# Part B of a fused attention and state-space kernel: queues written out by a list schedule, both magnitude tables of a chunk together, tiles laid out without shared ranges

## The chip, the cores and the metric

The kernel runs on one core of a Trainium2 chip. The metric is device time in microseconds (us) of one execution. The engines are TensorE (PE, with its weight loads as PEld), VectorE (DVE), ScalarE (ACT), GpSimd (POOL) and SyncE (SP, which here only issues DMAs). Each engine takes its instructions in the order of its own queue; an instruction that waits holds up all that stand behind it in the same queue.

## The reference, cut to what matters

Two independent parts are computed from their own inputs and laid side by side in the output (2048 rows, 640 + 640 columns).

```
part A (x: 2048 x 640, 32 heads of 20):
  q, k, v = x @ wqkv
  logits[s, w] = q[s] . k[s - 2w] / sqrt(20)      w = 0..7, masked where s < 2w
  out_a = softmax(logits) applied to v[s - 2w], then @ wo

part B (u: 2048 x 640, state size N = 192):
  dt = exp(log_dt);  K[d, l] = Re sum_n C[d,n] * exp(dt*A[d,n]*l) * dt*B[d,n]     l = 0..2047
  out_b = causal convolution of u with K along l, by an FFT of 4096  +  u * Dskip
```

## The kernel before, in words

Part B works on five chunks `c` of 128 channels. The start (`prep_dt`, `prep_coef`, `prep_chunk`) turns the parameters into logarithms and angles, splits them into pairs of half-precision pieces, writes these to a scratch tensor in memory (`scr`) and reads them back in another layout as PF (frequency pieces) and PM (magnitude pieces, `load_pieces`).

For each chunk and each half `th` of it, `table_steps` (L185) makes the powers exp(dt*A*l): PE multiplies the pieces by constant matrices into PSUM (L203, L206), and ACT turns each PSUM tile into a table. These are one small tile E (`gens`, Exp, L216), three tiles M (`mag`, Exp, L224), two tiles MX (`magx`, Exp, L238), and twelve tiles of 128 x 1024 for Y and X (`sin`, Sin, L252). Exp and Sin need different tables of ACT, and each change is an ACT_TABLE_LOAD. DVE multiplies M and MX by E (L229, L240), and Y and X by M and MX (L258 to L260, L264). M, MX and E have one buffer each; Y and X have one for each half.

`kgen_steps` (L274) then forms 16 of the chunk's 32 columns of K: 256 small matmuls into one PSUM tile (L290, L294), copied out by ACT (L297). With both halves done, `fwd_steps` does the forward transform of K (first stage L381, second stage L392). `prod` (L420) multiplies it by the transform of u, which the same `fwd_steps` made earlier and which lies in memory as `Ud`. `inv_steps` (L429) does the first inverse stage and stores it as `Zd`. Each step of these leaves a PSUM tile of 128 x 1024 that ACT or DVE copies to SBUF (L342, class `Evac`: a fixed pattern of letters says which engine takes which). Per chunk there are 20 such copies when a transform of u falls into it, and 2 of `kgen`.

The order comes from `interleave` (L347): it deals two lists of steps into each other in proportion to their lengths. One list is the table steps of the next half, the other what is left of this half: `kgen`, the inverse stage of the chunk before, and a forward transform. All PSUM tiles of part B come from one pool of four buffers of 128 x 1024 (tag `b`, L447). `InOrder` (L28) keeps a few chains of instructions in written order; for the rest the compiler's own scheduler orders each engine's queue.

The second inverse stage of part B (`ib`, L569) comes last, mixed with part A. It loads `Zd` back in groups of 12 of the 64 values of `l` (L575, five DMAs to a group, two buffers in turn) and multiplies by the constant H, loaded once (L564). Part A (`Attention`) starts within part B's last chunk: x is loaded and transposed (L637), then k and q of the first half are projected (L657) while the last chunk is finished. `Attention.run` (L796) does the rest: logits, softmax, the products with v (L772, L776) interleaved with `ib`, and the output projection (L790).

Of the kernel before, what the change touches and what calls it, by code (L numbers as in the profile page):

```python
# [10 lines left out]
A = mybir.AluOpType  # L11
# [7 lines left out]
NCH = 5  # L19
# [8 lines left out]
class InOrder:  # L28

    def __init__(self, tc):  # L30
        self.tc = tc; self.prev = None
    def __call__(self, ins):
        if self.prev is not None:
            self.tc.add_manual_dep(ins.ins, self.prev.name, mybir.DependencyInfo(mybir.DependencyClass.NoSync, mybir.DependencyReason.DATA), reason="act_order")
        self.prev = ins.ins
# [9 lines left out]
def load_dt(tc, pools, prm):  # L45
    nc = tc.nc
    pool = pools["arena"]
    ldt = pool.tile([128, NCH], bf16, name="ldt")
    lsrc = prm["B_log_dt"].rearrange("(g c t) -> g t c", g=4, c=NCH, t=32)
    for g in range(4):  # L50
        nc.scalar.dma_start(out=ldt[32 * g:32 * g + 32, :], in_=lsrc[g])
    return ldt


def prep_dt(tc, pools, ldt, order):
    nc = tc.nc
    pool = pools["arena"]
    dt = pool.tile([128, NCH], bf16, name="dt")
    order(nc.scalar.activation(out=dt[:], in_=ldt[:], func=ACT.Exp))
    dts = pool.tile([128, 3, NCH], f32, name="dts")  # L60
    nc.vector.tensor_scalar(out=dts[:, 0], in0=dt[:], scalar1=ASC, scalar2=None, op0=A.mult)
    nc.vector.tensor_scalar(out=dts[:, 1], in0=dt[:], scalar1=TURN, scalar2=None, op0=A.mult)
    order(nc.scalar.activation(out=dts[:, 2], in_=dt[:], func=ACT.Ln))
    return dts


def prep_coef(tc, pools, nat, lndt, n, order, vorder, T):

    nc = tc.nc
    V = nc.vector  # L70
    W = [128, n, CW]
    Br, Bi, Cr, Ci = (nat[:, a] for a in range(4))

    def zed():
        vorder(V.tensor_tensor(out=T[:, 0], in0=Br, in1=Cr, op=A.mult))
        vorder(V.tensor_tensor(out=T[:, 2], in0=Bi, in1=Ci, op=A.mult))
        V.tensor_tensor(out=T[:, 0], in0=T[:, 0], in1=T[:, 2], op=A.subtract)
        vorder(V.tensor_tensor(out=T[:, 1], in0=Br, in1=Ci, op=A.mult))
        vorder(V.tensor_tensor(out=T[:, 3], in0=Bi, in1=Cr, op=A.mult))
        V.tensor_tensor(out=T[:, 1], in0=T[:, 1], in1=T[:, 3], op=A.add)  # L80
        nc.scalar.activation(out=T[:, 2:4], in_=T[:, 0:2], func=ACT.Square)
        V.tensor_tensor(out=T[:, 4], in0=T[:, 2], in1=T[:, 3], op=A.add)

    def logs():
        order(nc.scalar.activation(out=T[:, 2:5], in_=T[:, 2:5], func=ACT.Ln, bias=pools["tiny"][:]))
        V.tensor_tensor(out=T[:, 3], in0=T[:, 3], in1=T[:, 2], op=A.subtract)
        V.scalar_tensor_tensor(out=T[:, 4], in0=T[:, 4], scalar=0.5, in1=lndt.unsqueeze(2).to_broadcast(W), op0=A.mult, op1=A.add)
        V.scalar_tensor_tensor(out=T[:, 2], in0=T[:, 3], scalar=-1.0, in1=T[:, 3], op0=A.mult, op1=A.max)

    def exps():  # L90
        order(nc.scalar.activation(out=T[:, 2], in_=T[:, 2], func=ACT.Exp, scale=-0.5))
        nc.scalar.activation(out=T[:, 3], in_=T[:, 3], func=ACT.Sign)
        nc.scalar.activation(out=T[:, 0:2], in_=T[:, 0:2], func=ACT.Sign, bias=pools["tiny"][:])

    def angle():
        ang = T[:, 2]
        order(nc.scalar.activation(out=ang, in_=ang, func=ACT.Arctan))
        V.scalar_tensor_tensor(out=ang, in0=ang, scalar=PI / 4, in1=T[:, 3], op0=A.subtract, op1=A.mult)
        V.scalar_tensor_tensor(out=ang, in0=ang, scalar=PI / 4, in1=T[:, 0], op0=A.add, op1=A.mult)
        V.scalar_tensor_tensor(out=ang, in0=ang, scalar=PI / 2, in1=T[:, 1], op0=A.subtract, op1=A.mult)  # L100
    return zed, logs, exps, angle, T[:, 4], T[:, 2]


def prep_chunk(tc, S1, S2, Are, Aim, dts, lam, ang, c, scr, vorder, sorder):


    nc = tc.nc
    V = nc.vector
    p = c % 2
    b1, tk, tq, b2 = S1[:, 3 * p:3 * p + 3], S1[:, 6], S1[:, 7], S1[:, 8]  # L110
    pc1, pc2, pc3 = (S2[:, 10 * p + a:10 * p + b] for a, b in ((0, 6), (6, 8), (8, 10)))
    so = sorder if sorder is not None else (lambda x: None)

    def frac(out, x, q):
        V.tensor_scalar(out=tk, in0=x, scalar1=1.0 / q, scalar2=MAGIC, op0=A.mult, op1=A.add)
        V.tensor_scalar(out=tk, in0=tk, scalar1=MAGIC, scalar2=q, op0=A.subtract, op1=A.mult)
        V.tensor_tensor(out=out, in0=x, in1=tk, op=A.subtract)

    def base():
        vorder(V.tensor_scalar(out=b1[:, 1], in0=Are, scalar1=dts[:, 0, c:c + 1], scalar2=-60000.0, op0=A.mult, op1=A.max))  # L120
        vorder(V.tensor_scalar(out=tq, in0=Aim, scalar1=dts[:, 1, c:c + 1], scalar2=None, op0=A.mult))
        frac(b1[:, 0], tq, 65536.0)
        frac(b1[:, 2], b1[:, 0], 1024.0)
        nc.scalar.copy(out=pc1[:, 0:3], in_=b1)
        vorder(V.tensor_tensor(out=pc1[:, 3:6], in0=b1, in1=pc1[:, 0:3], op=A.subtract))
        so(nc.sync.dma_start(out=scr[c, 0:6].rearrange("k p n -> p k n"), in_=pc1))

    def logmag():
        nc.scalar.copy(out=pc2[:, 0], in_=lam)
        vorder(V.tensor_tensor(out=pc2[:, 1], in0=lam, in1=pc2[:, 0], op=A.subtract))  # L130
        so(nc.sync.dma_start(out=scr[c, 6:8].rearrange("k p n -> p k n"), in_=pc2))

    def phi():
        V.tensor_scalar(out=tq, in0=b1[:, 0], scalar1=31.5, scalar2=None, op0=A.mult)
        V.scalar_tensor_tensor(out=tq, in0=ang, scalar=-TURN, in1=tq, op0=A.mult, op1=A.add)
        frac(b2, tq, 65536.0)
        nc.scalar.copy(out=pc3[:, 0], in_=b2)
        V.tensor_tensor(out=pc3[:, 1], in0=b2, in1=pc3[:, 0], op=A.subtract)
        so(nc.sync.dma_start(out=scr[c, 8:10].rearrange("k p n -> p k n"), in_=pc3))
    return base, logmag, phi  # L140


def new_pieces(tc, pools):


    nc = tc.nc
    PF = pools["arena"].tile([128, 8, CW], f16, name="PF", tag="PF", bufs=2)
    PM = pools["arena"].tile([128, 8, CW], f16, name="PM", tag="PM", bufs=2)
    nc.gpsimd.memset(PF[32:64], 0.0)
    nc.gpsimd.memset(PF[32:33], 4096.0)  # L150
    nc.gpsimd.memset(PM[64:128], 0.0)
    return PF, PM


def load_pieces(tc, P, scr, c, parts, sorder=lambda x: None):
    nc = tc.nc
    PF, PM = P
    where = {0: [(1, PM, 0), (4, PM, 1), (0, PF, 0), (3, PF, 1), (2, PF, 4), (5, PF, 5)], 1: [(6, PM, 2), (7, PM, 3)], 2: [(8, PF, 6), (9, PF, 7)]}
    for p in parts:
        for k, t, r in where[p]:  # L160
            sorder(nc.sync.dma_start(out=t[16 * r:16 * r + 16], in_=scr[c, k].rearrange("(g t) n -> t g n", t=16)))
# [22 lines left out]

def table_steps(tc, pools, R, P, th, order, Y, X, rows=(128, 128), vorder=None):  # L185

# [3 lines left out]
    nc = tc.nc  # L190
    V = nc.vector
    MM = nc.tensor.matmul
    RF, RM = R
    PF, PM = P
    pool, psp = pools["arena"], pools["psum"]
    M = pool.tile([128, 6400], bf16, name="M", tag="M", bufs=1)
    MX = pool.tile([128, 24, 32, 4], bf16, name="MX", tag="MX", bufs=1)
    E = pool.tile([128, 2, 24, 4], bf16, name="E", tag="E", bufs=1)
    steps = []

    def block(ps, blk, Pt, rhs, K=128):
# [7 lines left out]
    def new():  # L209
        return psp.tile([128, 2, 512], f32, name="ps_t", tag="b", bufs=4)  # L210

    def gens():
        ps = new()
        for blk in range(6):
            block(ps[:, 0, 32 * blk:32 * blk + 32], blk, PM, RM[:, 768:800], rows[0])
        order(nc.scalar.activation(out=E[:].rearrange("p k (b q) t -> p b k (q t)", b=6), in_=ps[:, 0, 0:192].rearrange("p (b k t) -> p b k t", k=2, t=16), func=ACT.Exp))  # L216

    def mag(b):
        def run():
            ps = new()  # L220
            for q in range(2):
                for i in range(2):
                    block(ps[:, q, 256 * i:256 * i + 256], 2 * b + i, PM, RM[:, 256 * q:256 * q + 256], rows[0])
# [8 lines left out]
    def magx(b0, n):  # L232
        def run():
            ps = new()
            for i in range(n):
                block(ps[:, i // 2, 256 * (i % 2):256 * (i % 2) + 256], b0 + i, PM, RM[:, 512:768])
# [656 lines left out]
```

## Time and profile before

| what | us |
|---|---|
| median of 3 runs (lowest, highest) | 533.36 (531.23, 533.85) |
| the profiled execution, whole | 537.6 |
| its span, first to last instruction | 535.8 |
| PE, DVE, ACT busy in the span | 391.0, 389.2, 345.4 |
| mean granted TensorE clock | 0.895 of full |

In this profile an instruction group is named by its line, engine, operation and tiles; "busy" is the union of its spans; "idle before" is time in which that engine stood still just before the group, with the instruction that ended it (the releaser). "issue" as a releaser means that the engine waited for nothing that the profile shows. A table of busy time by stretches of the span is the view that gives the stages: up to 52 us the start; 52 to 108 the first chunk; 108.17 to 344.20 the other four chunks; 344 to 383 the last transforms beside the first projections of part A; then part A with the last inverse stage.

### The profile page before, as it was taken

The page shows a single profiled execution, that of the slowest core. Times are in us where ns is not written, and L with a number is a line of the kernel's source. Part 1 is how long each engine was busy: PE and PEld are TensorE (multiplying, and loading weights), DVE is VectorE, ACT ScalarE, POOL GpSimd, SP SyncE. Part 2 cuts the span into 40 slices and gives each one's busy share as a digit, 9 for nine tenths or more (in the row PEclk, how much of TensorE's full clock was granted, in tenths as well). Part 3 has the DMA queues.
Part 4 walks back from the last instruction along what each step waited for, and adds up shares of the span by engine and source line. Part 5 has one row for each costly group of instructions (what it writes and reads, how often), then busy time and mean ns, then how long its engine had stood idle before and what let it go on. Part 6 is the DMA issues. An engine that isn't in the chain of part 4 may idle for free.

```text
span 535.8 us, 15507 instructions
## 1 busy us (share of the span) xinstructions
PE 391.0 (73%) x7009; PEld 245.8 (46%) x7009; DVE 389.2 (73%) x420; ACT 345.4 (64%) x451; POOL 35.9 (7%) x51
## 2 busy tenths in 40 slices
PE   0214675856798858976897678799799797788687
PEld 0103553533475436643564356445444465455355
DVE  3656997938878596989885977704585999985840
ACT  2393795957889868986998669557345362633254
POOL 8700001010002001010000000000000000000000
PEclk9999877878899887988799789989999799877879
DMA  5499343280028100750016008902102004653413
GB/s 122 107 156 220 115 139 84 94 195 3 1 67 260 31 0 18 234 166 1 3 44 196 1 2 295 241 22 80 80 1 62 1 4 113 188 123 103 102 67 107
DMA packets 51706, 51.57 MB, mean 96 GB/s; under 512 B 37416, under 2 KB 48360, under 8 KB 48696
## 3 DMA queue, kind: packets, MB, share of 16 engines
q1 hardware_dynamic: 49752, 49.69, 34.3%
q0 software_dynamic: 1184, 0.89, 0.8%
q8 instruction: 55, 0.90, 0.7%
q10 hardware_dynamic: 704, 0.00, 0.1%
q14 instruction: 11, 0.09, 0.1%
HBM read 32.30 MB, written 18.19 MB: 94 GB/s over the span
## 4 chain that ended last, share of the span: by engine, by line
DVE 36%; PE 34%; ACT 15%; issue 10%; DMA 4%; ACTq 0%; SPq 0%; POOL 0%; DVEq 0%; POOLq 0%
PE ps_qk L657 6%; DVE A L342 4%; DVE Y L258 4%; PE ps_t L203 4%; PE ps_k L290 4%; DVE X L264 3%; DVE prod L772 3%; PE ps_k L294 3%; DVE Y L260 3%; ACT Y L252 3%; PE ps_op L790 3%; PE ps_ia L429 2%; ACT X L252 2%; DVE Ssp L342 2%; DVE prod L713 2%
## 5 line engine op out<-in xcount | busy, mean ns | idle before, releaser
L252 ACT ACTIVATE X<-ps_t 128x1024 bf16<-128x1024 int16 x60 | 61.5, 1055 | 4.8 <-PE ps_t L203 3.3
L252 ACT ACTIVATE Y<-ps_t 128x1024 bf16<-128x1024 int16 x60 | 61.0, 1045 | 5.5 <-PE ps_t L203 3.5
L772 DVE TENSOR_TENSOR prod<-v,attn 128x2048 bf16<-128x2048 bf16 (+1 forms) x48 | 47.4, 1041 | 15.3 <-PE ps_o L776 15.3
L203 PE MATMUL ps_t<-R,PF 128*128 128x512 f16 (+1 forms) x160 | 52.0, 415 | 1.7 <-ACT Ksb L297 0.6
L713 DVE TENSOR_TENSOR prod<-qT,kT 128x5120 bf16<-128x5120 bf16 x16 | 44.6, 2817 | 9.1 <-ACT qT L342 4.7
L203 PE MATMUL ps_t<-R,PM 128*128 128x256 f16 (+3 forms) x160 | 22.9, 272 | 36.5 <-DMA PM<-scr 23.5
L258 DVE TENSOR_TENSOR Y<-Y,M 128x2048 bf16<-128x2048 bf16 x30 | 36.6, 1220 | 15.4 <-ACT Y L252 15.4
L342 DVE CAST A<-ps_f 128x1024 bf16<-128x1024 f32 x28 | 34.1, 1219 | 15.8 <-PE ps_f L381 15.8
L342 ACT CAST Ssp<-ps_f 128x1024 bf16<-128x1024 f32 x26 | 26.5, 1019 | 19.4 <-PE ps_f L392 19.4
L294 PE MATMUL ps_k<-Y,X 64*32 64x64 bf16 x1280 | 26.5, 235 | 16.5 <-issue 16.5
L264 DVE TENSOR_TENSOR X<-X,MX 128x2048 bf16<-128x2048 bf16 x30 | 36.6, 1219 | 0.2
L260 DVE TENSOR_TENSOR Y<-Y,M 128x2048 bf16<-128x2048 bf16 x30 | 36.6, 1218 | 0.2
L776 PE MATMUL ps_o<-prod,ident 32*32 32x512 bf16 (+1 forms) x768 | 24.1, 388 | 14.8 <-DVE prod L772 12.3
L381 PE MATMUL ps_f<-BD,u 128*64 128x128 bf16 x320 | 21.8, 290 | 17.5 <-DMA BD<-c_BD 12.0
L203 PEld LDWEIGHTS <-PM 128*128 128x128 f16 (+1 forms) x160 | 13.9, 102 | 44.4 <-DMA PM<-scr 23.5
L294 PEld LDWEIGHTS <-X 64*32 64x32 bf16 x1280 | 19.9, 116 | 30.1 <-issue 29.5
L381 PEld LDWEIGHTS <-u 128*64 128x64 bf16 x320 | 19.7, 204 | 25.5 <-issue 25.5
L224 ACT ACTIVATE M<-ps_t 128x1024 bf16<-128x1024 f32 x30 | 28.5, 1026 | 3.9 <-DVE Y L260 3.9
L420 DVE TENSOR_TENSOR U<-U,Ssp 128x2048 bf16<-128x2048 bf16 x20 | 24.3, 1221 | 9.0 <-ACT Ssp L342 9.0
L392 PE MATMUL ps_f<-A,WK 128*128 128x128 bf16 x160 | 16.5, 265 | 18.2 <-DVE A L342 18.2
L290 PE MATMUL ps_k<-Y,X 128*32 128x64 bf16 x1280 | 24.4, 242 | 5.7 <-ACT Ssp L342 1.9
L206 PE MATMUL ps_t<-R,PF 128*64 128x512 f16 (+1 forms) x160 | 27.4, 433 | 1.7 <-ACT Ssp L342 0.9
(146 smaller groups left out, 795.0 us busy)
## 6 DMA issues: line engine op xcount, KB each, us to landing
Udram<-Ssp SPq DMA_DIRECT2D x5, 1024.0 KB
U<-Udram SPq DMA_DIRECT2D x5, 1024.0 KB
U<-Udram SPq DMA_DIRECT2D x10, 512.0 KB
Zdram<-Z SPq DMA_DIRECT2D x5, 1024.0 KB
zq<-Zdram SPq DMA_DIRECT2D x25, 192.0 KB
u<-in_B_u_dram SPq DMA_DIRECT2D x4, 640.0 KB
xn<-in_A_x_dram SPq DMA_DIRECT2D x4, 640.0 KB
out_dram<-ob SPq DMA_DIRECT2D x16, 160.0 KB
```

Of the source, the lines that this page charges most:

```text
L203: MM(ps, lhsT=Pt[0:K, 2 * blk + th, 0:128], rhs=rhs[0:K], start=True, stop=True, skip_group_check=True)
L252: order(nc.scalar.activation(out=dst, in_=ps[:].bitcast(i16)[:, :, 0::2].rearrange("p i (k z) -> p (i k) z", z=128), func=ACT.Sin, scale=S ...
L258: V.tensor_tensor(out=hi, in0=lo, in1=m(0), op=A.mult)
L260: V.tensor_tensor(out=lo, in0=lo, in1=m(1), op=A.mult)
L264: V.tensor_tensor(out=xf, in0=xf, in1=mx, op=A.mult)
L290: MM(o, lhsT=X[:, r, 4 * g + t // 4, :, t % 4], rhs=Y[:, r, 4 * g + t // 4, :, t % 4], start=(k == 0 and r == 0), stop=False, tile_positio ...
L294: MM(o, lhsT=X[hb:hb + 64, r, kq, :, t % 4], rhs=Y[hb:hb + 64, r, kq, :, t % 4], start=False, stop=(r == 1), tile_position=(hb, 32 * g), s ...
L342: ins = self.nc.scalar.copy(out=out, in_=in_) if e == "a" else self.nc.vector.tensor_copy(out=out, in_=in_)
L381: MM(ps[64 * r:64 * r + 64, i], lhsT=src_fn(8 * q + i), rhs=BD[:, r], start=(i % 4 == 0), stop=True, skip_group_check=True, tile_position= ...
L657: self.nc.tensor.matmul(ps, lhsT=self.w[w][:, kt, 128 * ct:128 * ct + 128], rhs=rhs(kt), start=(kt == 0), stop=(kt == 4))
L713: self.nc.vector.tensor_tensor(out=pr[:], in0=self.qT[:, hf], in1=self.kT[:, hf, :, :, HALO - DIL * w:HALO - DIL * w + 256], op=A.mult)
L772: nc.vector.tensor_tensor(out=p2[:, 0:nd], in0=self.v2[b][:, :, off:off + 256], in1=self.attn[:, hf, w, :].unsqueeze(1).to_broadcast([128, ...
```

## The change

Part B and the start of part A are no longer emitted step by step. Each piece of work is entered in a plan as an operation with an engine (or a choice of two, ACT or DVE, for the PSUM copies), a duration written in the code, the keys that it reads and writes, and the PSUM tile that it uses. `Plan.schedule` then plays a clock: of all operations whose inputs are ready, it takes the one that can start first; among equals, the one with the smallest key (its number in program order plus an offset by kind). The instructions are emitted in that order, and `put` ties each to the one before it on its engine (PE, ACT, DVE, SP, POOL), so that every queue keeps it.

```
class Plan:
    LAG = dict(P=0.2, A=0.15, D=0.15, S=0.0, G=0.1, N=0.0)
    RATE = 150e3
...
    def put(self, e, ins):
        p = self.prev.get(e)
        if p is not None:
            self.tc.add_manual_dep(ins.ins, p.name, mybir.DependencyInfo(mybir.DependencyClass.NoSync, mybir.DependencyReason.DATA), reason="in_order")
...
    def evict(self, out, src, buf, width, w, r=(), eng="AD", kind=""):
        c = dict(A=0.1 + 0.0008 * width, D=0.08 + 0.00104 * width)
...
    def schedule(self):
...
                for e in o.eng:
                    c = o.cost[e] if isinstance(o.cost, dict) else o.cost
                    k = (max(t[e], at), o.key, c)
                    if best is None or k < best[0]:
                        best = (k, o, e, c)
...
            if o.func and o.func != table:
                c += 1.28; table = o.func
```

- **PSUM.** Instead of one pool of four there are two groups of two tiles: T for the tables, F for `kgen` and the transforms.
```
+        pl = Plan(tc, psk, dict(T=2, F=2))
```
- **Tables.** A chunk makes E once for both halves (32 matmuls of 16 columns instead of 2 x 8 of 32), then M and MX of both halves (two buffers each now), then the sines of half 0, then those of half 1. The table operations keep this order on ACT; in the start the magnitudes of both halves of chunk 0 come ahead of the arctangents, and a one-element Sin loads the table for these.
```
+                tb.gens()
+                tb.mags(0)
+                tb.mags(1)
...
+            tb.sins(0)
...
+            tb.sins(1)
```
- **Layouts.** Y, X, the intermediate A1 and the transform S are laid out with the block or quarter outermost, so that each copy writes a contiguous range of its own: A1 is `[4, 128, 8]` (was `[128, 32]` in columns of 8), S is `[4, 4, 8, 32]` (was `[4, 32, 32]`). The result of the first inverse stage goes through two tiles of a quarter (`Zs`) in place of one whole Z.
- **DMAs.** `Ud` and `Zd` are stored a quarter at a time (four DMAs in place of one); the pieces of a `Ud` store are 512 bytes, where a row was one piece of 8 KB. `Zd` is `[5, 128, 4, 128, 8]` in memory, so that a group load for `ib` has four pieces of 384 bytes to a partition where it had one of 1536. H is not loaded whole but with each group:
```
-                zt[0] = z = ar.tile([128, NCH, 2 * NP, 32], bf16, name="zq", tag=("X0", "S8")[l // NP % 2])
+                zt[0] = z = ar.tile([128, NCH + 1, 2 * NP * 32], bf16, name="zq", tag=("X0", "M0")[l // NP % 2])
+                nc.sync.dma_start(out=zt[3][:, 0:2 * np_], in_=Hd[:, 2 * l:2 * (l + np_)])
                 for c in range(NCH):
-                    nc.sync.dma_start(out=z[:, c, 0:2 * np_], in_=Zd[c, :, 64 * l:64 * (l + np_)].rearrange("p (m t) -> p m t", t=32))
+                    nc.sync.dma_start(out=zt[1][c], in_=Zd[c, :, :, 2 * l:2 * (l + np_)])
```
- **Smaller things.** u * Dskip is four operations on DVE instead of one. Load, transpose and first projections of part A are operations of the same plan. The constant BD is loaded ahead of u. `Attention.run` is the same, but for the names of the buffers that it uses again.

## The prediction

> **What bounds the kernel now.** I read the engine totals first, then the chain of work that ended last:
>
> ```profile
> PE 391.0 (73%) x7009; PEld 245.8 (46%) x7009; DVE 389.2 (73%) x420; ACT 345.4 (64%) x451; POOL 35.9 (7%) x51
> ...
> DVE 36%; PE 34%; ACT 15%; issue 10%; DMA 4%; ACTq 0%; SPq 0%; POOL 0%; DVEq 0%; POOLq 0%
> ```
>
> No engine is full over the span, and the chain passes between three of them. So I cut the span at the first Exp of each chunk. Columns: stretch, length, then busy time of PE, PEld, DVE, ACT, POOL, granted clock, DMA share, GB/s.
>
> ```profile
> 52.00:108.17 56.17, 39.98 (x588) 26.73 (x587) 51.64 (x99) 42.64 (x51) 3.09 (x3) 0.82 0.36 117
> 108.17:170.89 62.72, 46.59 (x896) 30.75 (x896) 46.51 (x46) 48.03 (x52) 4.55 (x4) 0.89 0.36 95
> 170.89:229.48 58.59, 46.26 (x896) 30.48 (x896) 46.05 (x46) 47.98 (x51) 4.28 (x4) 0.88 0.27 82
> 229.48:281.59 52.11, 41.23 (x800) 25.39 (x800) 45.90 (x42) 43.54 (x47) 0.93 (x1) 0.87 0.18 57
> 281.59:344.20 62.61, 47.51 (x894) 30.84 (x893) 49.07 (x50) 48.41 (x53) 0.00 (x0) 0.92 0.47 138
> ...
> 446.00:497.00 51.00, 39.58 (x1140) 25.28 (x1133) 41.96 (x41) 22.45 (x43) 0.00 (x0) 0.83 0.54 142
> ```
>
> The four chunks from 108.17 to 344.20 take 236.0 us, and in them PE is busy 181.6, DVE 187.5 and ACT 188.0: three equal loads, each idle for about 50 us. Nobody is the bound; the order is. The third shows what a better filled chunk looks like (DVE 45.90 of 52.11). What ended the idle times in that window, engine by engine (us, times, longest):
>
> ```profile
> DVE Z L342 <- PE ps_ia L429: 13.0, 4, 4.0
> DVE Y L258 <- ACT Y L252: 12.0, 5, 2.6
> DVE M L229 <- ACT M L224: 11.4, 7, 3.0
> DVE MX L240 <- ACT MX L238: 7.7, 2, 6.2
> ...
> ACT Ssp L342 <- PE ps_f L392: 18.4, 4, 4.7
> ...
> PE ps_f L392 <- DVE A L342: 18.2, 4, 4.7
> PE ps_k L294 <- issue: 12.9, 7, 4.9
> ```
>
> Two patterns stand out. At each half, DVE runs dry while ACT changes to Exp, makes the magnitudes, and changes back: 12.0 + 11.4 + 7.7 = 31.1 us. Once per chunk PE and ACT both stand for 4.6 us, because the four copies of the forward transform's first stage are all given to DVE, between its multiplications of the tables.
>
> **The change part by part.**
>
> *Table loads.* The trace has 24 of 1.283 us; in the window of the four chunks they are
>
> ```profile
> L216 ACT ACT_TABLE_LOAD x8 | 10.3, 1283 | 0.1
> L252 ACT ACT_TABLE_LOAD x8 | 10.3, 1283 | 0.1
> ```
>
> With both halves together a chunk has 2 in place of 4: 10.3 us less ACT work here, 2.6 in the first chunk. What one costs besides itself is seen where ACT goes on at once:
>
> ```profile
> 119.97 0.60 ACT L238 ACTIVATE MX<-ps_t 128x512 bf16<-128x512 f32 x1 [5.26 <-PE ps_t L206]
> 120.58 1.28 ACT L252 ACT_TABLE_LOAD   x1
> 121.88 1.02 ACT L252 ACTIVATE Y<-ps_t 128x1024 bf16<-128x1024 int16 x1
> ```
>
> From the end of one activation to the start of the next are 1.31 us. The Trainium skill (ScalarE: Activation LUTs, What ACT_TABLE_LOAD costs) states a drain of some 1.38 us on top, 2.66 us for a switch; by it the eight switches would save 21 us of ACT in place of 10.3, but this trace shows no such gap, and the measurement decides.
>
> *Magnitudes together.* One dry spell per chunk in place of two takes half of the 31.1 us: 15.6. M and MX have two buffers now, so ACT's waits for DVE to finish with M (3.9 us in the waits of ACT) go too, inside the same spells. Bounds: nothing, if the one spell is twice as long, and the whole 31.1, if transforms fill it. I take the half, since the DVE copies of the transforms can lie in it.
>
> *ACT or DVE by the plan.* Moving two of the four copies (1.13 us from start to start on DVE) to ACT, which stands idle then, takes 2.3 us out of each chunk, 9.2 in all; bounds 0 and 18.2. I take 9.2.
>
> *Sum for the four chunks:* 15.6 + 9.2 = 24.8 us; the table loads lie within the spells and are not counted again. 236.0 becomes 211. Cross-check: DVE and ACT together have 187.5 + 188.0 - 10.3 = 365 us, 183 each if shared evenly; PE has 181.6 plus the 12.9 us of "issue" in the kernel generation, which nothing here removes, 195. So 195 is the floor (-41), and 211 keeps PE at 92% of its time. The row against more is the third chunk's 88%.
>
> *First chunk.* Magnitudes of half 1 leave this stretch for the start: ACT loses 2.6 of loads and 4.8 of activations (3 of 1.03, 1.05, 0.59, 0.33), DVE 2.8 (2 of 0.95, one of 0.95). They fall into 40 to 50 us, where ACT is busy for 3.7 of 10 us. Left are DVE 48.8 and ACT 35.2; sharing the copies brings both to 42. At the 88% of the third chunk that is 48, 8 less than 56.17. Against it: the 4.8 us stand ahead of the arctangent (at 38.4 us), so the last pieces come back later; but the first X sine waits until 53.6 behind PE, which had stood 12.0 us for BD, loaded after u. I take -7 of the 8; without that cover it is -3; if the pieces come late as well, +4.
>
> *Last transforms and first projections (344 to 383):* PE is busy for 33.5 of 38.8 us; same work, slightly better packed: -2 (0 to -4).
>
> *Layouts.* Contiguous copies move the same elements; the 1.22 us of DVE and 1.02 of ACT stay. The gens' 16 more matmuls of 16 columns per chunk: those of 32 columns go four in 0.24 us, so +0.5 us of PE per chunk at most, inside the 16 us of PE slack that 211 leaves. For the transform's S and the moving data of `ib`, now in runs of 8 elements, no row exists; bounds from 0 to twice the 16.2 us of `ib` matmuls, whose PE is busy 39.6 of 51. I take 0.
>
> *DMAs.* The quarter stores add 15 issues for `Ud`, 15 for `Zd` and 5 for H to SP. A `u` load of 2048 pieces takes 2.6 us to issue, so 512 pieces 0.65: 13 us for `Ud` over the run, on a queue idle most of the time; behind them stand the `U` loads and the pieces of the next chunk, wanted some 20 us later. Cost 0. A `Zs` tile comes free when its store has landed; a store of 288 KB took 4.1 us at the start, so two tiles allow a quarter every 2 us; the copy that waits holds its ACT or DVE queue. I take 0, up to +2 per chunk.
>
> *Loads for `ib`.* Here the change costs. A group was 0.98 MB and is 1.18 with H, in pieces of 384 bytes. The rows: the first group in pieces of 1536 bytes, and u in pieces of 320 bytes:
>
> ```profile
> 448.50:453.80 5.30, 3.02 (x70) 1.44 (x62) 5.27 (x7) 0.58 (x1) 0.00 (x0) 1.00 0.69 194
> ...
> 37.00:45.00 8.00, 0.00 (x0) 0.00 (x0) 5.30 (x12) 5.08 (x7) 0.00 (x0) 1.00 1.27 146
> ```
>
> At 146 GB/s a group takes 8.1 us, at 194 it was 5.1. `ib` uses one up in 4 x 46/22 = 8.4 us, so later groups are just covered; the first adds 3.0 to PE's wait, with `av` queued behind it and DVE behind that. In all, 5.2 + 1.0 MB of groups and 2.6 of output are 8.9 MB, 61 us at 146 GB/s against the 51 us of the stretch. Bounds 0 and +10; the u row is nearest in piece size, but part of the output falls behind the last `ib`; I take +4. The Trainium skill (DMA: Bandwidth & Descriptors, Specifications) names 512 bytes as the least for line rate. By it the `Ud` pieces are free and these are not; it gives no price, and the rows do.
>
> **The sum.** -7 - 25 - 2 + 4 = -30. The profiled span of 535.8 becomes 506, its execution of 537.6 (1.8 lies around the span) 507.6. That execution is 4.2 above the median, and I carry this over: 503.4, say 504.
>
> **Rivals.**
>
> 1. *The plan reaches the floor* (15%): chunks at 195, first chunk -11, tail -3, loads 0: -55, 478. For it: three equal loads are easy to overlap. Against it: the third chunk's 88%, and PE's clock, 0.87 to 0.92 already.
> 2. *The order gains little* (14%): the spells last as long as before since M waits for Exp all the same, the plan's order differs from the old one in names, and only table loads and start gain: -10 -7 +8 for the loads at their worse end: -9 or less, 524 to 533.
> 3. *PSUM takes the place of the order* (17%), slower. F has two tiles for 20 copies and 2 generations a chunk; all four served everything before. A transform step holds a tile for 1.05 (16 matmuls) + 1.1 (copy) + some 0.4 of hand-over, 2.6; a generation for about 8. That is 68 us of tile per chunk, 34 with two tiles, plus 11 times the mean wait of a full tile for its copy. A chunk of 53 allows 1.7 us of wait; 59, as now, is reached at 2.3; with 2.7 it is 64, the four chunks 256: +20 +4 -7 = +17, 550. ACT and DVE at 90% with operations of 1.0 to 1.2 us can make a copy wait two turns. Against it: the plan sees the tiles and may choose either engine.
>
> **Chances and range.** The forecast (490 to 522) has 54%. Faster by over 0.5% (about what a measurement of this kernel can tell from no change): 54 + 15 + most of rival 2, 10: 79%. Within it: 4%. Slower: 17%. The range 480 to 545 leaves out half of rival 1 and half of rival 3.
>
> **What would show it.** Table loads: 24 become 13. The spells: DVE's idle before M and MX falls to half of 19. The copies: PE's 18.2 us before L392 are gone, and ACT has more of the A copies. Chunks: 53 us from Exp to Exp, PE idle mostly by "issue". Loads: PE waits for `zq` 3 us or more. PSUM: PE's idle time released by copies of F tiles. I am wrong if chunks stay near 59, or if the start loses more than it gains.

## The result and the profile after

The changed kernel takes 529.8 us (median of 20 runs, 527.85 to 532.75), beside 533.92 for the kernel before on the same chip (20 runs): a ratio of 0.9923, 95% interval [0.9903, 0.9943]. That is 4.1 us less, where 30 were forecast. The profiled span is 528.5 us, 7.3 less than before.

The page of the changed kernel, engine totals and the chain that ended last:

```profile
PE 396.1 (75%) x7089; PEld 254.1 (48%) x7089; DVE 378.7 (72%) x417; ACT 340.3 (64%) x442; POOL 21.9 (4%) x41
...
PE 40%; DVE 28%; issue 11%; ACT 10%; DMA 7%; POOL 3%; SPq 1%; DVEq 0%; ACTq 0%; POOLq 0%
```

DVE's share of the chain fell by 8 points, as the change meant it to; PE's rose by 6 and the DMAs' by 3. The stretches from Exp to Exp of chunks 1 to 3, then chunk 4, then the last transforms with the first projections, last the same stretch of the final inverse as was shown of before (columns as there):

```profile
103.01:157.93 54.92, 46.09 (x976) 31.13 (x976) 45.59 (x46) 46.26 (x50) 0.00 (x0) 0.91 0.33 88
157.93:211.53 53.60, 42.99 (x816) 29.45 (x814) 42.16 (x42) 43.20 (x47) 0.00 (x0) 0.94 0.30 85
211.53:270.09 58.56, 50.14 (x1037) 35.54 (x1038) 49.51 (x50) 49.54 (x54) 0.00 (x0) 0.91 0.33 99
270.09:316.00 45.91, 38.75 (x788) 24.62 (x791) 42.10 (x42) 41.37 (x44) 0.00 (x0) 0.93 0.22 74
316.00:370.58 54.58, 42.33 (x537) 27.77 (x526) 16.26 (x17) 27.32 (x41) 0.66 (x4) 0.91 0.30 97
446.00:497.00 51.00, 38.19 (x1044) 24.63 (x1036) 34.34 (x35) 20.23 (x42) 0.00 (x0) 0.78 0.62 141
```

Chunk 4 is packed better than any chunk of before (ACT and DVE over 90%), the three ahead of it are not, and the 54.58 us behind have PE busy for 42.33. PE's waits over the whole changed kernel (us, times, longest) say what stands there:

```profile
PE ps_F L63 <- issue: 14.8, 5, 4.2
PE ps_T L63 <- DMA PF<-scr: 10.9, 5, 4.7
...
PE ps_F L63 <- DVE A L69: 6.9, 8, 2.1
```

Two of PE's waits in the kernel before:

```profile
PE ps_f L392 <- DVE A L342: 23.5, 6, 4.7
PE ps_k L294 <- issue: 16.5, 9, 4.9
```

The wait for DVE's copies, 23.5 us over the span of before, is down to 6.9. A wait for the pieces (PF) is new: none of before's waits names it. The "issue" is nearly as long as before.

By stage, between the first Exp of chunk 1, that of chunk 4 and part A's first product (us; the last two rows are experiments told below):

| | start to chunk 1 | chunks 1 to 3 | chunk 4 to part A | part A | span |
|---|---|---|---|---|---|
| before | 108.2 | 173.4 | 100.8 | 153.4 | 535.8 |
| forecast of the change | -7 | -19 (three quarters of 25) | -8 (-6 and -2) | +4 | 506 |
| after | 103.0 (-5.2) | 167.1 (-6.3) | 100.5 (-0.3) | 157.9 (+4.5) | 528.5 |
| true keys | 98.9 | 159.2 | 100.4 | 156.8 | 515.2 |
| true keys, U small | 98.1 | 146.8 | 93.8 | 156.3 | 495.0 |

The stretches don't hold quite the same work: in chunks 1 to 3 PE does 2592 multiplications before and 2821 after, while the busy times of DVE and ACT differ by 1.2 us at most.

### The profile page after: what moved, and what is told of

The parts are those of the page before. It is cut to its first block, busy times and chain, and to the rows that moved or that the text cites. A ratio compares the mean times of both kernels' runs of the same rounds, so it can differ in the third digit from the quotient of the medians.

```text
span 528.5 us, 15725 instructions
## 1 busy us (share of the span) xinstructions
PE 396.1 (75%) x7089; PEld 254.1 (48%) x7089; DVE 378.7 (72%) x417; ACT 340.3 (64%) x442; POOL 21.9 (4%) x41
## 4 chain that ended last, share of the span: by engine, by line
PE 40%; DVE 28%; issue 11%; ACT 10%; DMA 7%; POOL 3%; SPq 1%; DVEq 0%; ACTq 0%; POOLq 0%
PE ps_F L63 16%; PE ps_T L63 13%; DVE prod L984 4%; DMA PF<-scr 3%; DVE A L69 3%; DVE Y L72 3%; PE ps_op L1002 3%; PE ps_qk L876 3%; DVE prod L925 3%; DVE U L72 3%; PE ps_ib L772 2%; POOL natr L81 2%; PE ps_o L988 2%; DVE X L72 2%; ACT M L66 2%
## 5 line engine op out<-in xcount | busy, mean ns | idle before, releaser
L63 PE MATMUL ps_T<-R,PF 128*128 128x512 f16 (+3 forms) x320 | 81.3, 441 | 24.6 <-DMA PF<-scr 10.9
L66 ACT ACTIVATE X<-ps_T 128x1024 bf16<-128x1024 int16 x60 | 61.3, 1038 | 21.1 <-PE ps_T L63 20.1
L63 PE MATMUL ps_T<-R,PM 128*128 128x256 f16 (+7 forms) x400 | 40.9, 260 | 32.4 <-DMA PM<-scr 24.3
L63 PE MATMUL ps_F<-Y,X 128*32 128x64 bf16 (+1 forms) x2560 | 53.4, 238 | 14.9 <-issue 14.8
L66 ACT ACTIVATE Y<-ps_T 128x1024 bf16<-128x1024 int16 x60 | 60.3, 1039 | 4.6 <-PE ps_T L63 3.5
L63 PEld LDWEIGHTS <-X 128*32 128x32 bf16 (+1 forms) x2560 | 39.5, 116 | 39.4 <-issue 32.4
L925 DVE TENSOR_TENSOR prod<-qT,kT 128x5120 bf16<-128x5120 bf16 x16 | 44.6, 2817 | 15.4 <-ACT qT L69 12.2
L66 ACT ACTIVATE M<-ps_T 128x1024 bf16<-128x1024 f32 x30 | 30.0, 1028 | 5.0 <-PE ps_T L63 4.2
L69 DVE CAST A<-ps_F 128x1024 bf16<-128x1024 f32 x22 | 26.7, 1219 | 7.6 <-PE ps_F L63 7.6
L1002 PE MATMUL ps_op<-wo,o 128*128 128x320 bf16 x160 | 27.0, 331 | 0.7 <-ACT o L992 0.7
L63 PE MATMUL ps_F<-IA,U 128*128 128x128 bf16 x320 | 26.9, 233 | 0.3 <-DVE A L69 0.2
L72 DVE TENSOR_TENSOR M<-M,E 128x1536 bf16<-128x1536 bf16 x20 | 18.5, 954 | 10.9 <-ACT M L66 10.9
```

The costliest lines, as they stand in the source:

```text
L63: return self.put("P", self.nc.tensor.matmul(out, **kw))
L66: return self.put("A", self.nc.scalar.activation(**kw))
L69: return self.put(e, self.nc.scalar.copy(out=out, in_=in_) if e == "A" else self.nc.vector.tensor_copy(out=out, in_=in_))
L72: return self.put("D", self.nc.vector.tensor_tensor(**kw))
L925: self.nc.vector.tensor_tensor(out=pr[:], in0=self.qT[:, hf], in1=self.kT[:, hf, :, :, HALO - DIL * w:HALO - DIL * w + 256], op=A.mult)
L1002: self.nc.tensor.matmul(ps[:], lhsT=self.o4[:, hf, sc, dd, s0:s0 + 128], rhs=self.wo[:, dd, 320 * eh:320 * eh + 320], start=(dd == 0), sto ...
```

## The experiments

Each was run beside the kernel before on its own chip, so ratios to before are compared where a per cent matters.

### 1. The wait that the plan didn't know

In the changed kernel PE stops amid the X sines of chunk 2. PE's timeline (start, duration, what, idle before and releaser):

```profile
200.91 0.66 PE L63 MATMUL ps_F<-Y,X 64*32 64x64 bf16 x32
206.23 1.06 PE L63 MATMUL ps_T<-R,PF 128*64 128x512 f16 x4 [4.66 <-DMA PF<-scr]
```

and SP's queue of the same kernel at that moment:

```profile
201.01 0.33 SPq L81 DMA_DIRECT2D PF<-scr  x1
```

The load brings pieces of chunk 4 into the PF buffer that chunk 2 still reads. The X multiplications take all 128 rows of PF (the constant rows that meet rows 0 to 31 are zero), but the keys in the plan name rows 64 to 127 alone. So the plan put the load of rows 0 to 31 ahead of the last X multiplications, and these, which do read those rows, had to wait until it landed. ACT then stood for 5.3 us behind PE.

**e1: true keys.**
```
-        pf = self.pf(0) if which == 0 else self.pf(2) + self.pf(3)
+        pf = self.pf(0) if which == 0 else self.pf(0) + self.pf(2) + self.pf(3)
```


> The plan is told that the multiplications for X read all rows of PF, so the pieces of the chunk after next are written only behind them. Theory: PE's five waits for PF, 10.9 us in the trace of the changed kernel, are one that the plan did not know, and they go: 520 to 524 us, no wait of PE for PF after the start. Rival (the place of the wait is taken by another, PE or PSUM being the bound): 528 to 531 us, with the waits gone all the same.

Measured: 519.45 us, ratio 0.973 [0.9689, 0.9771], 10.4 us below the changed kernel. No wait for PF is left in the trace. ACT and DVE do their work in the same order as in the changed kernel, so it is not another plan that gains. The sum of these waits, 10.9, is what their absence gave: shown.

### 2. Three steps of the prediction, undone one at a time

**e2: magnitudes of the second half back between the sines** (`tb.mags(1)` moved to stand before `tb.sins(1)` in chunks 1 to 4).

> The magnitudes of half 1 come right ahead of its sines again in chunks 1 to 4, the plan and all else kept: 8 more table loads. Theory of the prediction (a second dry spell per chunk, 15.6 us for four chunks): 540 to 546 us. Rival (the plan fills the spells with transforms, so that only the order matters): 529 to 533 us.

Measured: 531.64 us, 0.9972 [0.9938, 1.0006]; 1.8 us lost by the medians, 2.6 by the ratios (the intervals just overlap), not 15.6.

**e3: one PSUM group** (`dict(T=2, F=2)` becomes `dict(T=4)`).

> All PSUM tiles of the plan from one group of four, as before the change. Rival of the prediction (two tiles for the transforms are what holds the new order up): 5 us or more faster, below 525 us. Theory (the split is not what costs): 527 to 533 us.

Measured: 529.53 us, 0.9915 [0.9887, 0.9943]: the split costs nothing.

**e4: the first copies of K's transforms on DVE alone** (`eng="D"` for A of K).

> The four copies of the first stage of the forward transform of K go to DVE alone, as before the change in all chunks but the last. Step of the prediction (2.3 us per chunk): 537 to 541 us, and PE waits for these copies again. Rival (the plan moves other work off DVE instead): 529 to 533 us.

Measured: 529.75 us, 0.9909 [0.9874, 0.9945]: nothing lost.

So neither of the two steps that made up the forecast's 25 us shows in the changed kernel. They could be hidden by other waits, so they come again in part 4. The PSUM groups (e3) were not tried again without those waits.

### 3. PE's stands by "issue"

In the true-keys kernel PE's stands in part B all lie in the busy stretch of the DMA queues that a load of U begins. PE's timeline, then what the DMA queues carried from 143.2 to 147.0 (packets, MB, share of the 16 engines):

```profile
143.28 0.22 PE L63 MATMUL ps_F<-Y,X 128*32 128x64 bf16 x1
146.87 0.68 PE L63 MATMUL ps_F<-Y,X 128*32 128x64 bf16 x31 [3.38 <-issue]
```
```profile
q1 hardware_dynamic: 1352, 1.05, 96.5%
q8 instruction: 1, 0.02, 1.7%
```

The 31 multiplications belong to a run of 32 equal ones; PE needs nothing new for them but the instructions. In the whole execution the queue called "instruction" (q8) moved 55 packets, 0.90 MB, some 16 KB each, and one of them moved during this stand.

Where in PE's own sequence do the stands fall? The trace has 14,229 records of PE (7089 multiplications, 7089 weight loads, 51 others), which is 55.6 times 256. Counted in the order of their starts, with the packets of q8 beside them, the five stands of the true-keys kernel in part B are:

| PE goes on at (us) | number of the record | records since the stand above | packet of q8 began, after PE had entered the 256 records ahead (us) | packet landed, before PE goes on (us) |
|---|---|---|---|---|
| 146.87 | 3009 | | 5.7 | 1.5 |
| 197.97 | 4801 | 7 x 256 | 4.8 | 1.4 |
| 250.49 | 6594 | 7 x 256 + 1 | 5.1 | 1.4 |
| 307.70 | 8642 | 8 x 256 | 3.1 | 1.4 |
| 316.09 | 8898 | 1 x 256 | 5.9 | 1.4 |

Each stand falls where one block of 256 ends, and PE goes on soon after the next packet has landed. Where no data moved in between, the packet began at most 1.1 us after PE had entered the block ahead; here it came late, at DMA shares of 0.98 to 1.07. Over the traces of all twenty kernels, the one before among them, 72 of 73 stands by "issue" of 0.85 us and more (outside the last inverse) lie at this place of the count, to within 2. The experiments that follow ask what makes the packet late.

**e9: U's loads for chunks 1 to 4 left out** (the call of `uload(c + 1)` removed).

> The version with the X multiplications' true keys (519.45 us), and the loads of U for chunks 1 to 4 left out (four times 2 MB; the products then multiply into what lies in U, so part of the data is wrong). In that version's trace PE stands 9.2 us by "issue" in chunks 1 to 3 (3.4, 2.4 and the like) and 6.3 + 2.7 us at 305 to 316 us, and each of these stands lies inside the 6 us or more in which a U load keeps the DMA engines at 330 to 400 GB/s. Theory A: PE's next instructions come over the same DMA engines and queue behind the U load. Without the loads PE's idle by "issue" before the groups on F falls from 16.1 us to under 6, and the time by about as much: 508 to 513. Rival B: the stands belong to the many small matmuls (K = Y times X, 64x64) themselves; they stay, and the time stays at 517 to 521.

Measured: 502.93 us, 0.9403 [0.9327, 0.9479]. 16.5 us gone, more than expected; one stand of 2.6 is left.

**e13: the same order, U's loads small** (8 of 128 rows, in `uload`).

> The version with true keys (519.45 us), its order of instructions unchanged on every engine, but the loads of U for chunks 1 to 4 cut to 8 of 128 rows (0.13 MB instead of 2 MB each; the products of the other rows multiply into what lies there). Leaving the loads out took 16.5 us away, but let the plan reorder too. Theory A (the loads' traffic holds up PE's instructions): nearly all of it comes back with the old order, 502 to 507, and PE stands at most 4 us by "issue" before the groups on F instead of 16.1. Rival B (most of the gain was the plan's new freedom): 510 to 518.

Measured: 501.11 us, 0.9388 [0.9336, 0.944]. With the order of instructions kept, it is the traffic that makes the stands. Chunks 1 to 3 with U whole, then small, in one row each:

```profile
98.86:258.04 159.18, 137.74 (x2815) 95.83 (x2812) 137.91 (x138) 138.90 (x149) 0.00 (x0) 0.95 0.35 96
```
```profile
98.05:244.89 146.84, 132.98 (x2817) 93.31 (x2815) 137.05 (x138) 138.23 (x148) 0.00 (x0) 1.00 0.21 64
```

The stands there sum to 9.2 us, the stretch is 12.3 shorter. The other part is in the first number after the length: PE does the same multiplications in 4.8 us less, and the granted clock is 1.00 instead of 0.95 (PE's other waits grew by 1.6). A stand is paid twice here, once while PE waits and once while its clock is low.

**e15: U loaded later, whole.** In the plan U's load now comes after the next chunk's magnitudes:
```
             if c < last:
-                uload(c + 1)
...
+                tb = tabs(c + 1); tb.gens(); tb.mags(0); tb.mags(1)
+            if c:
+                uload(c, [pl.funcs[-1]])
```


> The version with true keys, with U's load (whole, 2 MB) planned after the next chunk's magnitudes instead of at once when the last inverse has read U: from about 134 us to about 163 us in chunk 1, where PE runs some 11 multiplications a microsecond instead of 35, so that what it has fetched lasts longer, and where no writes of Ud queue beside it. Theory A: the three stands of 2.4 to 3.4 us in chunks 1 to 3 shrink to half or less, and the product starts no more than 4 us later: 510 to 516. Rival B: the product, now waiting for the load, holds up the K transform's buffers as much: 518 to 525.

Measured: **503.30 us, 0.942 [0.9379, 0.9462]**, all data computed: the fastest full version here, faster than both kernels. One stand of 2.0 us is left. The load is no smaller; it runs in another place. The plan also deals the other work in another order than in e1, so the 16.1 us are not the place's alone; e13, with the order kept, gives 18.3 for the traffic. Rows of the true-keys kernel, where it falls into the K multiplications:

```profile
132.00:138.00 6.00, 6.00 (x163) 3.99 (x162) 6.00 (x7) 5.64 (x7) 0.00 (x0) 1.00 0.79 206
138.00:144.00 6.00, 5.50 (x156) 3.26 (x153) 5.90 (x7) 5.77 (x8) 0.00 (x0) 1.00 0.99 223
144.00:147.00 3.00, 0.13 (x12) 0.13 (x15) 2.68 (x4) 0.89 (x1) 0.00 (x0) 0.85 1.02 308
...
147.00:150.00 3.00, 3.00 (x84) 1.42 (x84) 0.87 (x1) 1.08 (x2) 0.00 (x0) 0.58 0.26 74
```

and of the version with U late, where it falls among the sines:

```profile
162.00:165.00 3.00, 2.38 (x34) 1.93 (x32) 2.35 (x3) 3.00 (x5) 0.00 (x0) 1.00 1.06 371
165.00:168.00 3.00, 2.73 (x41) 2.27 (x39) 1.92 (x3) 3.00 (x5) 0.00 (x0) 1.00 0.99 214
```

The DMA share (last but one column) is about 1 at the stand in the first and in both rows of the second. In the first, PE had run 26 to 27 multiplications a microsecond (163 in 6.00), each with its weight load, and stopped; in the second it runs 11 to 14 and doesn't. (The first rows are of 6 us, the others of 3.)

The Trainium skill (Runtime: NRT & Kernel Launch, Instruction fetch mechanics) says that an engine's instructions come in blocks of 256 over a DMA queue of its own, and that crossing a block is mostly hidden. The 55 packets of 16 KB and the place of the stands agree with the first; the stands of 2.4 to 3.6 us speak against the second while the DMA engines are full. An estimate from that page: at 27 multiplications and 27 weight loads a microsecond a block lasts 4.7 us, at 11 and 11 it lasts 11.6, longer than the whole load. In the traces the block ahead of the stand at 146.87 lasted 4.9 us, and the one that the same load of U meets in e15 lasted 14.1 (155.7 to 169.8).

So PE waits for its next 256 instructions, whose packet comes late behind data: the place of the stands and the packets' times show the first, e13 the second. The load does no harm in e15's place because the block that runs beside it outlasts it.

**e21: U late, but the keys as in the change.**

> The kernel after the change, its keys for X left as they are, with U's load planned after the next chunk's magnitudes. Theory A (the two losses are separate and add): 529.8 - 16 = 514, 511 to 517. Rival B (the plan, given the load's new place, puts the pieces' loads elsewhere, or the waits for pieces overlap with the stands, so that one hides the other): 520 to 528.

Measured: 517.59 us, 0.9697 [0.9666, 0.9727]; 12.2 below the changed kernel, between the two ranges. PF waits of 9.3 us remain. So three quarters of U's price show while the other loss is still there.

**e17: the inverse first**, which brings U's load forward (`I=-200, Ie=-200` among the plan's offsets).

> The version with true keys, with the last inverse stage of part B's chunks given a higher priority in the plan, so that U comes free and is loaded earlier, in chunk 4 ahead of x and of wv. Theory A (the stands come where loads pile up during the K multiplications): chunk 4's two stands of 2.7 and 3.6 us shrink, the others move little: 513 to 517. Rival B: the earlier inverse takes PE from the tables, and the time stays or rises: 519 to 524.

Measured: 525.59 us, 0.9834 [0.9781, 0.9887], 6 slower than true keys alone. Five stands, 13.9 us in all, remain; chunks 1 to 3 take 159.8 us as before the edit (159.2), and chunk 4 to part A 106.5 where it was 100.4. Rival B's direction, beyond its range, and its reason isn't shown.

**e12: U in quarters.** 

> The version with true keys (519.45 us), with U of chunks 1 to 4 loaded in four quarters, each with its own keys, so that each starts when the last inverse stage has read that quarter, instead of 2 MB at once (same bytes, 12 issues on SP a chunk instead of 3, pieces of 512 bytes). Theory A (PE's instructions queue behind the load): the backlog is shorter at any time, the stands by "issue" shrink by half, 513 to 517. Rival B (the stands have nothing to do with the load, or the shorter pieces and more issues cost as much): 518 to 523.

Measured: 539.92 us, 1.011 [1.0045, 1.0174]. The edit isn't what it says: every step of the last inverse reads part of each quarter, so quarters were loaded before the inverse had read them, values are mixed, and PE waits for loads in between. Its 17.4 us of PE's waits for U hide whatever else it does. It tells nothing on the theory.

**e20: the kernel before, U small** (the same cut in `load`, one U tile for all chunks).

> The kernel before, with U's loads for chunks 1 to 4 cut to 8 of 128 rows (the other rows multiply into what lies there). Its PE stands 16.2 us by "issue" within the table chunks and behind, nearly as long as after the change. Theory A: the stands cost the kernel before as much, so that it falls by 12 to 17 us, to 517 to 522, and the change did not bring them. Rival B: before, PE had to wait for other engines there anyway, and the time falls by 5 us at most, to 529 to 534; then the change's tighter order made the stands count, and they are part of its loss.

Measured: 532.60 us, 0.9976 [0.9954, 0.9999]: 0.8 us. The time is rival B's, the reason is neither's: the stands in chunks 1 to 3 of the kernel before are still there, 10.3 us, so U had not made them. In the kernel before U's load and the stand lie in different places:

```profile
160.00:163.00 3.00, 3.00 (x37) 2.02 (x37) 2.98 (x4) 2.71 (x4) 0.00 (x0) 1.00 1.01 418
163.00:166.00 3.00, 2.33 (x32) 1.50 (x30) 2.97 (x4) 2.85 (x3) 0.00 (x0) 1.00 1.05 322
...
172.00:175.00 3.00, 3.00 (x132) 2.35 (x124) 0.77 (x1) 2.61 (x5) 0.00 (x0) 1.00 1.01 350
175.00:178.00 3.00, 0.69 (x33) 0.52 (x32) 1.83 (x2) 1.66 (x2) 0.00 (x0) 1.00 0.31 62
178.00:181.00 3.00, 3.00 (x76) 1.37 (x72) 0.96 (x1) 2.51 (x3) 0.00 (x0) 0.57 0.03 5
```

U came at 157 to 169, with 10 to 12 multiplications a microsecond: no stand. The stand at 176 comes behind the store of a whole `Ud` (1 MB, issued at 170.9, with loads of pieces right behind it), with 44 a microsecond, and it too lies at the end of a block of 256. That the store makes it late was not tried by itself. So the change cut the store into quarters, and moved U's load out of a harmless place into the K multiplications.

### 4. The prediction's steps again, without the losses

**e10: true keys, magnitudes apart.** 

> The version with true keys (519.45 us), with the magnitudes of the second half of chunks 1 to 4 put back between the two halves' sines (8 more table loads). Alone on the change this cost 1.8 us, while the waits for the pieces were still in the way. Theory A: those waits hid it; without them it costs what the prediction gave, half of it at least: 527 to 535. Rival B: the magnitudes together are worth little even then, since eight table loads of 1.3 us fall on ACT, which has 12 to 13 us per chunk in hand: 519 to 523.

Measured: 515.01 us, 0.9649 [0.9599, 0.9699]: 4.4 *faster* than together. It has 13.6 us of PE stands of 0.9 us and longer where true keys alone has 18.9 (3.3 and 3.5 of these in the last inverse): the loads fell into other places.

**e18: the same with U small.** 

> The version with true keys and U's loads cut to 8 rows (501.11 us: neither waits for pieces nor stands under U's load; the other rows multiply into what lies there), with the magnitudes of the two halves of chunks 1 to 4 apart again. Theory A (magnitudes together are worth what the prediction gave, and the losses hid it): half of 15.6 us at least is lost, 509 to 517. Rival B (eight more table loads are hidden on ACT, and nothing else hangs on it): 500 to 504.

Measured: 506.18 us, 0.948 [0.9447, 0.9513], against 0.9388 [0.9336, 0.944] together. So with neither loss in the way, the magnitudes together are worth some 5 us, up to 8 if the one stand of 2.9 that e13 has and e18 hasn't is added: a third to a half of the 15.6.

**e16: U late and magnitudes apart.** 

> As the run before with the magnitudes of the two halves of chunks 1 to 4 apart too, so that U's load is planned after the first half's magnitudes. Apart alone on the true keys gave 515.01 us, 4.4 below the version together, with 11.4 us of PE stands by "issue". Theory A (both work): 507 to 513. Rival B (apart was faster only because it happened to move the loads to other places, so nothing adds): 514 to 519.

Measured: 511.32 us, 0.9572 [0.9529, 0.9615]. Theory A's range, but for a poor reason: against 503.30 it is 8.0 slower, and it has 11.0 us of stands against 2.0. The largest, 4.8 us, ends at 315.6, behind the loads of U and wv and the stores of Zd issued from 303 on.

**e11: true keys, copies on DVE.** 

> The version with true keys (519.45 us), with the K transforms' first copies (A) on DVE alone instead of by the plan on ACT or DVE. Alone on the change this cost nothing. Theory A (the prediction's 2.3 us a chunk, masked by the waits for the pieces): 526 to 530. Rival B: the plan moves other copies to ACT in their place, and nothing is lost: 518 to 521.

Measured: 517.69 us, 0.9709 [0.9649, 0.977]: no loss.

**e19: U late, copies on DVE.** 

> The version with true keys and U's load late (503.30 us, whole data), with the K transforms' first copies on DVE alone. Theory A (the prediction's 9.2 us for the free choice, hidden so far): 508 to 513. Rival B: the plan gives ACT other copies instead, and the time stays at 502 to 505.

Measured: 519.32 us, 0.9715 [0.9673, 0.9757]: 16.0 lost, more than any theory said. 7.7 of it are stands (9.7 against 2.0), since the plan's new order puts U's load of chunk 3 at 251 us:

```profile
251.00:254.00 3.00, 3.00 (x116) 2.18 (x112) 3.00 (x4) 2.66 (x4) 0.00 (x0) 1.00 1.00 265
...
257.00:260.00 3.00, 2.04 (x62) 1.31 (x59) 2.88 (x3) 2.53 (x3) 0.00 (x0) 1.00 0.98 213
260.00:263.00 3.00, 0.22 (x16) 0.22 (x17) 0.00 (x0) 0.00 (x0) 0.00 (x0) 1.00 0.22 52
```

39 multiplications a microsecond beside a full DMA, and three engines stand. The copies' own price can't be read from this run; what else makes up the other 8 us stays open.

### 5. The loads for the last inverse

**e22: zq in long pieces** (`Zd` read as it lies, 1536 bytes a piece). 

> The version with true keys and U's load late (503.30 us), with zq of the last inverse loaded in long contiguous pieces of Zdram (1536 bytes; same bytes, but other values than the stage needs, which it multiplies in another order). Theory A (the short pieces keep the DMA engines busy at a share of 0.67 from 404 to 450 us and make PE late for the prod stages): the DMA share falls by a third there, PE's wait for zq (3.6) goes, and so do 3 to 6 us: 497 to 501. Rival B: PE is late because its clock falls to 0.67 at 430 to 450 and because it holds more work, and the loads are early enough: 502 to 505.

Measured: 496.74 us, 0.928 [0.9236, 0.9324]: theory A's time, but not its signs (the DMA share from 404 to 450 fell from 0.68 to 0.60, and PE's wait for `zq` rose).

**e24: H loaded twice instead of six times.** 

> The version with true keys and U's load late (503.30 us), with H loaded only for the first two groups of the last inverse and used again for the others (leaves out four of six loads of H; the others use the wrong part of H). Theory A (the reloads of H, 1 MB, crowd the queue): 1 to 3 us less, 500 to 502. Rival B (they lie ahead of their use and cost nothing): 502.5 to 505.

Measured: 496.79 us, 0.9294 [0.9238, 0.9351]: more than either theory said.

Either gives some 7 us against 0.942. From part A's first product to the end are 162.4 us with U late, 158.3 with long pieces and 157.6 with H loaded twice: 4 to 5 us lie in this stage, the rest ahead of it, where these edits change nothing. The last inverse's multiplications, with U late and then with long pieces (shortest, median, longest ns; first and last start), then PE's waits for `zq` with U late, long pieces, H twice:

```profile
L772 PE MATMUL ps_ib<-zq x512: 224/231/336, 418.1 to 458.0; 32*32 32x160 bf16 x171
```
```profile
L772 PE MATMUL ps_ib<-zq x512: 224/312/337, 414.6 to 452.4; 32*32 32x160 bf16 x171
```
```profile
PE ps_ib L772 <- DMA zq<-Zdram: 3.6, 1, 3.6
```
```profile
PE ps_ib L772 <- DMA zq<-Zdram: 4.9, 2, 2.8
```
```profile
PE ps_ib L775 <- DMA zq<-Zdram: 0.4, 1, 0.4
```

With long pieces they end 5.6 us earlier (2.1 of it gained ahead of part A), although PE's wait for `zq` is longer; with H loaded twice that wait nearly goes. So the loads set the pace of this stage by way of more than the wait that carries their name. Since either cure alone gives it all, it seems to be the sum of pieces and H that was too much for the queues; that is argued, not shown.

## Why the prediction was wrong, step by step

- **The direction and the sum.** Faster, as forecast; 4 us in place of 30. The version with true keys and U late has 503.30, beside a forecast of 504, but by other terms than the forecast's: that the two numbers meet is luck. Where the rest of its gain in chunks 1 to 3 comes from no run separates; before's own stands there, 10.3 us, and its low clock, 0.88, are gone from it.
- **"DMAs. ... Cost 0": the step that failed most.** It counted SP's issues and asked whether data would come in time. It didn't ask what a load in a new place does to others. The pieces' loads cost 10.4 us by a key that the plan lacked (e1), and U's load among the K multiplications 16 to 18 (e15, e13).
- **"Issue" as a fixed 12.9 us "which nothing here removes".** Wrong: it is PE waiting for its next 256 instructions, it depends on what the DMA engines carry, and it went to 2.0 (e15). Nor did the same transfers make it before and after, though its length was alike. Before, U had no part in it.
- **"Magnitudes together", 15.6.** 5 to 8 without the losses (e18), 1.8 to 2.6 in the change itself (e2). DVE's idle time before M and MX in chunks 1 to 3 did fall, from 15.1 to 7.3 us, as the text asked to see, and the 24 table loads did become 13. But DVE's whole idle time there fell only from 34.9 to 29.8 (173.42 - 138.47, 167.08 - 137.26): waits for PE's transforms took its place, and behind these the PF waits and stands. Half of an idle time was taken for half of a gain.
- **"ACT or DVE by the plan", 9.2.** PE's wait for DVE's A copies fell from 13.6 to 4.5 in chunks 1 to 3, and ACT has 18 of the 40 A copies where it had 12. The sign that was asked for came, the time didn't (e4, e11); e19 can't be read for it.
- **Cross-check, floor 195 (48.8 a chunk).** With both losses gone three chunks take 146.8, 48.9 each (e13), but the number is met by luck. The floor held 12.9 us of "issue" as fixed; e13 has none there, and PE is busy for 133.0 of the 146.8. In e15 three chunks take 140.6, under the floor (with 2593 multiplications in the stretch, not 2817).
- **First chunk, -7.** -5.2; with true keys -9.3, since 3.9 us of PF waits fell into the change's first chunk. About right.
- **Chunk 4 and last transforms, -6 and -2.** -0.3. The last sine of chunk 4 starts some 25 us earlier than before (314.9, not 339.7), but two stands (2.9 and 3.8 us, from 318 and 325) meet the loads of U and wv at DMA shares of 1.07 and 0.90, and behind the tables PE has most of the work. Without U's traffic it is -7.
- **Loads for `ib`, +4.** Part A grew by 4.5, and easing the loads gives 4 to 5 there where all else is out of the way (e22, e24). The size was right. The sign, PE waiting 3 us for `zq`, came too: the changed kernel has one wait of 3.3 in the last inverse, against 0.8 before. The list of waits calls it "issue", but it does not lie at the end of a block of 256, the view of the tile `zq` puts it down to `zq`, and so does the list at the same multiplications in e15 (3.6). That the loads are all of the 4.5 in the change was not tried.
- **Rivals.** PSUM fell (e3: 529.53 with one group, beside 529.8). The second, "the order gains little", gave 524 to 533 and holds the time, but named another cause: the spells did shrink.

## What to carry to other kernels

A planner is as right as its keys: compare what each operation truly reads, rows that meet zeros too, with the keys it names, and look in the trace after for a wait on a transfer that the plan held to be free. Look at where each large load falls, not only whether it is in time: beside a run of many small matmuls full DMA engines stopped PE, beside fewer, larger ones they did not. The sign is idle "issue" on PE amid equal matmuls; whether it is the fetch of instructions can be seen by counting PE's records and looking for stands that are multiples of 256 apart. And an idle time that goes is a gain only as far as nothing stands next in line; before it is counted, each other engine's waits in that stretch are to be read too.

## What the runs showed of the hardware

- PE's stands by "issue" lie whole multiples of 256 of PE's instructions apart, and PE went on 1.4 to 1.5 us after a 16 KB packet of the queue "instruction" had landed (true keys, five stands of 2.4 to 3.6 us). With the DMA engines full that packet began 3.1 to 5.9 us after PE had entered the block ahead, with no data moving at most 1.1 us after.
- In the rows shown with the DMA share near 1, PE at 26 to 44 matmuls a microsecond (each with a weight load) came to a stand; in those with 11 to 14 it did not.
- The granted clock was 0.58 in the 3 us after a stand of 3.38 us (row 147 to 150 above) and 1.00 after that. The Trainium skill (TensorE: Matmul & The Clock Gate, The HAM clock gate) states half clock after an idle window of some 3.4 us; the row agrees. In the kernel before, a stand of 2.31 us was followed by 0.57 as well (row 178 to 181), so less than such a window was enough there.
